# Scaling attention values in place for three of four head pairs, by GpSimd, instead of turning, scaling and turning back every block

## The chip, the cores and the metric

The kernel runs on one core of one Trainium2 chip. The metric is the device time of one execution in microseconds (us). The engines are named as in the profile: PE is TensorE (PEld its weight loads), DVE is VectorE, ACT is ScalarE, POOL is GpSimd, SP is SyncE, whose queue (SPq) issues all the DMAs of this kernel. Each engine works through its own instructions in the order in which they stand; between engines there are only semaphores.

## What is computed

There are 8 batches, 8 heads, 576 positions and 64 columns a head. Each head's attention keeps the 32 largest scores of a row, and its result goes, head beside head, into a mixer of width 512:

```python
scores = scale * np.matmul(q, k.transpose(0, 1, 3, 2))
kth = np.partition(scores, -top_k, axis=-1)[..., -top_k:-top_k + 1]
scores = np.where(scores >= kth, scores, -1000000000.0)
attn = np.exp(scores - np.max(scores, axis=-1, keepdims=True))
attn = attn / (np.sum(attn, axis=-1, keepdims=True) + 1e-09)
x = np.matmul(attn, v)            # then (B, S, H * D)
theta = x @ w_theta
zr, zi = x * np.cos(theta), x * np.sin(theta)
y = np.einsum('ts,bsd->btd', w_tok_r, zr) + np.einsum('ts,bsd->btd', w_tok_i, zi)
u = x + y
out = u + np.maximum(u @ w_ch, 0.0)
```

The division by the row's sum is what the change moves: both kernels multiply the values `attn @ v`, computed with unscaled weights, by the reciprocal of the sum.

## The kernel before

**Units.** Two heads make a pair; a batch has four pairs. A pair is worked on in five units, `j` = 0 to 4: four of 128 query rows for both heads, and a last one of the remaining 64 rows of both heads, which lie one under the other in the 128 partitions. For a unit the scores are made on PE (`scores`), copied by ACT, folded in two and searched for the 32nd largest value by DVE (`fold`, `pick`, `threshold`: rounds of MAX8 and MATCH_REPLACE8 on a list `lst`, of which there are three). POOL makes the limits from the list (`lim`, line 303) and a copy for a later check (`marks`, line 305); ACT makes a penalty (`pen`, line 311), POOL subtracts it (line 313), ACT takes the exponential with the row's sum (line 323), PE turns the result (`turn`), and PE multiplies it with the values (`mix_values`), which ACT keeps in `xt` (`keep_values`, line 378). `xt` has columns of heads in its 128 partitions (a pair for each of its four blocks) and the 576 positions along the row.

**The pipeline.** `pipeline` runs over 160 units, one step for each, and in each step it touches several neighbouring units at different stages. The loads of the next pair (`load_pair`, `split_pair`: `raw`, `hi`, `q`, `kh`, `kl`, `vt`, `vrem`) are written at the first two steps of a pair. All of it is then put in order by a scheduler, engine by engine, which works with its own estimates of durations; the program's text gives the priorities.

**The mixer.** When the last unit of a batch is kept, its `mixer` starts, a generator that is taken on by a few pieces in each step beside the units of the next batch; that of the last batch (with `split` set, in which PE works with high and low halves of its operands) has nothing beside it at the end. In its front part the sums have to be applied. A row's sum lies in the partition of its query position, while `xt` has the positions along the row. So for each block k of 128 positions (five, the last of 64) PE turns the four blocks of `xt` (`px_s`, line 542), DVE multiplies them by the reciprocals `rinv` into `xs` (`normalize`, line 443), and PE turns `xs` back (`px_t`, line 458), from where ACT copies it to `xt` (`turn_back`, line 459). `xs` is needed turned in any case, for the products with cosine and sine. Then come the angles (`angles`, PE, `pth`), their fraction (`fraction`), sine and cosine on ACT (`trig`), the products by POOL (lines 506 and 511), the matmuls over positions (`py`, line 585), and those over columns (`po`, line 610). The exponential and the sine need different tables on ACT, so that no exponential runs between the first sine and the last cosine of a mixer.

The reciprocals are made at the mixer's start from `sums` of all heads, [128, 5, 8], after POOL and ACT have moved the sums of the last units to the right partitions (lines 411 and 412), by DVE (lines 415 and 416).

Of the kernel before, what the change touches and what calls it, by code (L numbers as in the profile page):

```python
# [22 lines left out]
AHEAD = 2  # L23
S_LATE = 0
# [19 lines left out]
def topk_attention_phase_mixer(  # L44
# [33 lines left out]
    ps_m = ctx.enter_context(tc.tile_pool(name="ps_m", bufs=2, space=bass.MemoryType.PSUM))  # L78

# [10 lines left out]
    nc.gpsimd.memset(marks[:, :, 1:], 0.0)  # L90
    factors = const.tile([P, 1, 2], F32, name="factors")
# [287 lines left out]


# [28 lines left out]
    def mixer(bt, split=False):  # L409
        bq, xt, sums, sums_rem = bt["bq"], bt["xt"], bt["sums"], bt["sums_rem"]  # L410
        nc.gpsimd.tensor_copy(sums[:REM, NJ, 0::2], sums_rem[0:D])
        nc.scalar.copy(sums[:REM, NJ, 1::2], sums_rem[D:P])
        rinv = wk2.tile([P, NJ + 1, H], F32, tag="rinv", name="rinv")
# [23 lines left out]
        def normalize(k, px):  # L437
            rows, parts = (P, 1) if k < NJ else (REM, folds)
            for a in range(parts):
                cols = slice(a * DM // parts, (a + 1) * DM // parts)  # L440
                out = xs[a * D : a * D + rows, k, : DM // parts]
                hs = slice(cols.start // D, cols.stop // D)
                nc.vector.tensor_tensor(
                    out.rearrange("p (h d) -> p h d", d=D),
                    px[:rows, cols].rearrange("p (h d) -> p h d", d=D),
                    rinv[:rows, k, hs].unsqueeze(2).to_broadcast([rows, hs.stop - hs.start, D]),
                    op=ALU.mult,
                )

        def turn_back(j):  # L450
            rows, parts = (P, 1) if j < NJ else (REM, folds)
            m = NB // parts
            for a in range(parts):
                sl = slice(a * D, a * D + rows)
                pt = ps_t.tile([P, NB, P], F32, tag="t", name="px_t")
                with later(M_PE):
                    for p in range(m):
                        nc.tensor.transpose(pt[:, p, :rows], xs[sl, j, p * P : p * P + P], ident[sl, sl])
                nc.scalar.copy(xt[:, a * m : a * m + m, j * P : j * P + rows], pt[:, :m, :rows])  # L459
                if split:  # L460
                    cs = slice(j * P, j * P + rows)
                    nc.scalar.copy(x_hi[:, a * m : a * m + m, cs], pt[:, :m, :rows])
                    for p in range(a * m, a * m + m, 2):
                        pp = slice(p, p + 2)
                        nc.vector.tensor_sub(x_lo[p // 2][:, :, cs], xt[:, pp, cs], x_hi[:, pp, cs].bitcast(F32))
# [22 lines left out]
        def fraction(j):  # L488
            whole = wk2.tile([P, DM], F32, tag="whole", name="whole", bufs=1)
# [46 lines left out]
        for k in range(NJ + 4):  # L536
# [245 lines left out]
```

## Time and profile before

| | us |
|---|---|
| median of 3 runs | 1294.06 |
| lowest and highest | 1293.27 and 1298.52 |
| the profiled execution | 1298.9 |
| its span, from the first to the last instruction | 1297.1 |

| engine | busy, us | share of the span |
|---|---|---|
| PE | 1168.7 | 90% |
| DVE | 1165.8 | 90% |
| ACT | 1018.5 | 79% |
| POOL | 663.1 | 51% |

The profile is of the one execution, and it is 4.8 us above the median. The ends of matmuls are modelled, so that PE's busy time holds some overlap of one matmul with the next. A batch takes about 150 us: the tables of the exponential are loaded at 233.8, 380.6, 529.1, 681.7, 830.4, 981.5 and 1129.7 us, at the end of the sine and cosine of each batch but the last. The last mixer, alone, begins at about 1215 us.

### The profile page before, as it was taken

The numbers are of one execution on the slowest core, as the hardware profiler recorded it, in microseconds if no ns is written. First come the engines' busy times: TensorE is split into PE (matmuls) and PEld (weight loads), VectorE is DVE, ScalarE is ACT, GpSimd is POOL, SyncE is SP. The second block draws the span as 40 slices with busy tenths as digits, with TensorE's granted clock in tenths as the row PEclk, the third lists the DMA queues.
The fourth block names the chain that finished last, engine by engine and source line by source line (L and its number), as shares of the span: only waits on it lengthen the run. The fifth ranks groups of instructions, "written<-read, shape, count | busy, mean of one in ns | idle before, by whom it ended". The sixth has DMA issues, their size and how long they took to land.

```text
span 1297.1 us, 21711 instructions
## 1 busy us (share of the span) xinstructions
PE 1168.7 (90%) x6293; PEld 852.4 (66%) x6293; DVE 1165.8 (90%) x3993; ACT 1018.5 (79%) x2098; POOL 663.1 (51%) x784
## 2 busy tenths in 40 slices
PE   3676688899989999999989998899988999999998
PEld 3554455678657775578656775577756786577688
DVE  7999999999988899999998899999998799999353
ACT  5998888987788688787779778977778778887560
POOL 3667765654465345544455435554464444655440
PEclk9676789999999999899999999999999999999999
DMA  6244532322412342313413333123423233220001
GB/s 177 83 132 130 149 100 56 91 76 84 126 36 56 83 129 74 80 40 92 135 48 74 83 110 92 36 67 90 128 56 81 58 95 103 72 60 11 37 2 39
DMA packets 71008, 106.04 MB, mean 82 GB/s; under 512 B 13920, under 2 KB 32608, under 8 KB 70880
## 3 DMA queue, kind: packets, MB, share of 16 engines
q1 hardware_dynamic: 70880, 104.57, 29.5%
q8 instruction: 52, 0.85, 0.3%
q14 instruction: 76, 0.62, 0.2%
HBM read 38.40 MB, written 9.44 MB: 37 GB/s over the span
## 4 chain that ended last, share of the span: by engine, by line
DVE 32%; PE 32%; ACT 22%; POOL 4%; SPq 3%; issue 3%; DMA 3%; ACTq 0%; DVEq 0%; POOLq 0%
PE py L585 11%; DVE lst L292 10%; DVE lst L298 9%; PE pth L481 6%; PE px L366 4%; ACT e L323 4%; ACT pen L311 4%; DVE lst L274 3%; DVE lo L275 3%; DVE lst L279 3%; ACT e L252 3%; PE ps_score L243 3%; SPq L211 3%; ACT at L340 3%; PE pt L338 2%
## 5 line engine op out<-in xcount | busy, mean ns | idle before, releaser
L313 POOL TENSOR_TENSOR e<-e,pen 128x576 f32<-128x576 f32 x288 | 365.3, 1286 | 195.2 <-ACT pen L311 184.3
L292 DVE MAX8 lst<-lst 128x8 f32<-128x296 f32 (+3 forms) x1152 | 424.1, 406 | 0.9
L298 DVE MATCH_REPLACE8 lst<-lst 128x277 f32<-128x277 f32 (+2 forms) x864 | 329.2, 386 | 0.0
L585 PE MATMUL py<-w,z 128*128 128x288 f32 x1008 | 270.4, 412 | 0.0
L323 ACT ACTIVATE e<-e,lim 128x576 f32<-128x576 f32 x288 | 225.7, 786 | 34.7 <-POOL e L313 33.7
L311 ACT ACTIVATE pen<-e,lim 128x576 bf16<-128x576 f32 x288 | 211.0, 776 | 37.0 <-POOL lim L303 37.0
L243 PE MATMUL ps_score<-kh,q 128*128 128x288 f32 x512 | 186.3, 378 | 56.4 <-DVE lo L275 30.9
L585 PEld LDWEIGHTS py<-w,z 128*128 128x128 f32 x1008 | 184.7, 192 | 52.8 <-issue 5.4
L338 PE MATMUL pt<-ident,e 128*128 128x128 f32 x1152 | 176.8, 287 | 29.5 <-ACT at L340 15.0
L338 PEld LDWEIGHTS pt<-ident,e 128*128 128x128 f32 x1152 | 139.5, 146 | 71.2 <-ACT at L340 18.8
L366 PE MATMUL px<-at,vt 128*64 128x320 f32 (+1 forms) x1024 | 174.9, 440 | 4.5 <-ACT at L343 4.5
L252 ACT COPY e<-ps_score 128x576 f32<-128x576 f32 x256 | 163.1, 650 | 10.7 <-PE ps_score L243 10.2
L340 ACT COPY at<-pt 128x512 f32<-128x512 f32 x256 | 145.0, 589 | 29.5 <-PE pt L338 28.5
L243 PE MATMUL ps_score<-kl,q 128*128 128x288 f32 x512 | 155.4, 318 | 1.3 <-DMA kl<-raw 1.3
L243 PEld LDWEIGHTS ps_score<-kh,q 128*128 128x128 f32 x512 | 103.1, 201 | 77.7 <-DVE lo L275 28.1
L274 DVE TENSOR_TENSOR lst<-ps_score,e 128x576 f32<-128x576 f32 (+1 forms) x160 | 109.5, 685 | 47.8 <-ACT e L252 22.1
L366 PEld LDWEIGHTS px<-at,vt 128*64 128x64 f32 x1024 | 77.8, 145 | 72.2 <-issue 26.4
L610 PE MATMUL po<-xt,w 128*128 128x288 f32 x448 | 118.7, 408 | 0.7 <-DVE xt L566 0.3
L279 DVE MAX8 lst<-lo 128x8 f32<-128x288 f32 x288 | 116.6, 440 | 0.0
L481 PE MATMUL pth<-w,xt 128*128 128x512 f32 x224 | 107.3, 624 | 5.6 <-ACT xt L459 5.6
L275 DVE TENSOR_TENSOR lo<-ps_score,e 128x576 f32<-128x576 f32 (+1 forms) x160 | 109.5, 684 | 0.0
L243 PEld LDWEIGHTS ps_score<-kl,q 128*128 128x128 f32 x512 | 104.2, 204 | 7.1 <-issue 2.0
(120 smaller groups left out, 1689.1 us busy)
## 6 DMA issues: line engine op xcount, KB each, us to landing
kh<-hi SPq DMA_DIRECT2D x124, 144.0 KB, 2.7
kl<-raw SPq DMA_DIRECT2D x124, 144.0 KB, 2.6
raw<-in_qT_dram SPq DMA_DIRECT2D x31, 288.0 KB, 3.0
raw<-in_kT_dram SPq DMA_DIRECT2D x31, 288.0 KB, 3.1
q<-hi SPq DMA_DIRECT2D x62, 144.0 KB, 2.5
q<-raw SPq DMA_DIRECT2D x62, 144.0 KB, 2.7
vt<-in_v_dram SPq DMA_DIRECT2D x32, 256.0 KB, 2.8
out_dram<-ot SPq DMA_DIRECT2D x28, 288.0 KB, 2.1
```

Source lines behind the costliest of these rows:

```text
L243: nc.tensor.matmul(out[:, at : at + n], l, r, start=(i == 0), stop=(i == len(mm) - 1), skip_group_check=True)
L252: nc.scalar.copy(u.x[:, :, keys], u.ps[:, :, :HS])
L292: nc.vector.max(lst[:, w, best], part[w])
L298: nc.vector.match_replace(out=rest, in_to_replace=lst[:, w, best], in_values=part[w], imm_value=LOWEST)
L311: nc.scalar.activation(pen[:, w], u.x[:, w], AF.Relu, bias=u.lim[:, w, 0:1], scale=-STEEP)
L313: nc.gpsimd.tensor_sub(u.x[:, w], u.x[:, w], pen[:, w])
L323: nc.scalar.activation(u.x[:, w], u.x[:, w], AF.Exp, bias=u.lim[:, w, 1:2], scale=SCALE, accum_out=acc)
L338: nc.tensor.transpose(pt[:, c], e[:, w, at0 : at0 + P], ident)
L340: nc.scalar.copy(at[:, w, :, q0 : q0 + P], pt)
L366: nc.tensor.matmul(px[sl, :n], pr["vt"][:, kb, sl], pr["at"][:, a, kb], start=(kb == 0), stop=False, skip_group_check=True)
L481: nc.tensor.matmul(th[j][: l.shape[-1]], l, r, **pos)
L585: nc.tensor.matmul(py[:, :HS], l, r, start=(i == 0), stop=(i == len(mm) - 1))
```

## The change

For pairs 0, 1 and 2 of a batch the reciprocals are made beside the units of the next pair, and `xt` is scaled where it lies. `spread`, two steps after a pair's last unit: POOL adds 1e-9 to the pair's sums [128, 9], DVE takes the reciprocal, PE turns the 9 columns into rows, ACT copies these (`line`), three DMAs write them to memory as two rows of 576 (`away`), and two DMAs read each row back into 64 partitions (`wide`). `scale`, four steps after a pair's last unit: POOL multiplies the pair's block of `xt` [128, 576] by `wide` in place.

In the mixer only pair 3 is turned, multiplied by DVE and turned back (`turn_last`, `turn_back`). The other three pairs are turned once, for `xs`, and copied by ACT (`turn_values`). The fraction of the angles shares a buffer with the output `ot`. The mixer has nine pieces up to its sines' end, where it had ten.

```diff
+SPREAD = 4
+    far = ctx.enter_context(tc.tile_pool(name="far", bufs=2, space=bass.MemoryType.DRAM))
+    small = const.tile([P, 2 * NJ + 1], F32, name="small")
+    nc.vector.memset(small, 1e-9)
...
-            if j < NJ:
-                acc = bt["sums"][:, j, 2 * p + w : 2 * p + w + 1]
-            else:
-                acc = bt["sums_rem"][:, p : p + 1]
+            if j == 0 and w == 0:
+                bt["sums"][p] = wk2.tile([P, 2 * NJ + 1], F32, tag="sums", name="sums")
+            c = w * NJ + j if j < NJ else 2 * NJ
+            acc = bt["sums"][p][:, c : c + 1]
...
+    def invert(bt, p):
+        rinv = wk2.tile([P, 2 * NJ + 1], F32, tag="rinv", name="rinv")
+        nc.gpsimd.tensor_add(rinv, bt["sums"][p], small)
+        nc.vector.reciprocal(rinv, rinv)
+        return rinv
+    def spread(bt, p):
+        rinv = invert(bt, p)
+        pr = ps_t.tile([P, NJ * P], F32, tag="t", name="pr")[: 2 * NJ + 1, :P]
+        nc.tensor.transpose(pr, rinv, ident)
+        row = wk2.tile([2 * NJ + 1, P], F32, tag="line", name="line", bufs=1)
+        nc.scalar.copy(row, pr)
+        away = far.tile([2, S], F32, tag="away", name="away")
+        for w in range(2):
+            nc.sync.dma_start(away[w, : NJ * P].rearrange("(j q) -> j q", q=P), row[w * NJ : w * NJ + NJ])
+        nc.sync.dma_start(away[:, NJ * P :].unsqueeze(0), row[2 * NJ :].rearrange("o (w q) -> o w q", w=2))
+        wide = wk2.tile([P, S], F32, tag="wide", name="wide", bufs=1)
+        for w in range(2):
+            nc.sync.dma_start(wide[w * D : w * D + D], away[w].partition_broadcast(D))
+        bt["wide"][p] = wide
+    def scale(bt, p):
+        nc.gpsimd.tensor_mul(bt["xt"][:, p], bt["xt"][:, p], bt["wide"][p])
...
-        for rows, js in ((P, slice(0, NJ)), (REM, slice(NJ, NJ + 1))):
-            nc.vector.tensor_scalar(rinv[:rows, js], sums[:rows, js], 1e-9, None, op0=ALU.add)
-            nc.vector.reciprocal(rinv[:rows, js], rinv[:rows, js])
+        rinv = invert(bt, lp)
+        rrem = wk2.tile([P, 2], F32, tag="rrem", name="rrem")
+        nc.gpsimd.tensor_copy(rrem[:REM, :1], rinv[:D, 2 * NJ :])
+        nc.scalar.copy(rrem[:REM, 1:], rinv[D:, 2 * NJ :])
...
+        def turn_values(k):
+            rows = P if k < NJ else REM
+            px = ps_t.tile([P, DM], F32, tag="t", name="px_s")
+            with later(M_PE):
+                for p in range(lp):
+                    nc.tensor.transpose(px[:rows, p * P : p * P + P], xt[:, p, k * P : k * P + rows], ident)
+            if k < NJ or split:
+                nc.scalar.copy(xs[:rows, k, : lp * P], px[:rows, : lp * P])
...
+            for p in range(lp):
+                halve(u_hi[p], u_lo[p], xt[:, p], nc.scalar.copy, nc.vector.tensor_sub)
+        turn_last()
+        yield
+        turn_back()
+        turn_values(0)
+        yield
+        for k in range(NJ + 2):
             if k <= NJ:
...
+                angles(k)
+            if k < NJ:
+                turn_values(k + 1)
+            if k:
+                fraction(k - 1)
...
+            for gone, act in ((2, spread), (SPREAD, scale)):
+                u = unit(i - gone)
+                if u and u.j == NJ and u.p < NPAIR - 1:
+                    act(u.batch, u.p)
```

Line numbers of the changed kernel are four higher from the units on, and more in the mixer: the subtraction of the penalty is line 313 before and 317 now, `lim` 303 and 307, `marks` 305 and 309. Two places show what moved. The first is PE at the front of a batch's mixer, beside the scores (`ps_score`) of the next batch's first pair. Before, turning (`px_s`) and turning back (`px_t`) alternate, block by block:

```order
L542 MATMUL px_s<-ident,xt 128x128 x4
L458 MATMUL px_t<-ident,xs 128x128 x4
L243 MATMUL ps_score<-kh,q_6599 128x288
L243 MATMUL ps_score<-kl,q_6599 128x288
L243 MATMUL ps_score<-kh,q_6599 128x288
L243 MATMUL ps_score<-kl,q_6599 128x288
L338 MATMUL pt<-ident,e 128x128 x8
```

Now, at the same mixer, pair 3 is turned and turned back once for all blocks:

```order
L473 MATMUL px_s<-ident,xt 128x128 x4
L473 MATMUL px_s<-ident,xt 64x128
L247 MATMUL ps_score<-kh,q_6730 128x288
L247 MATMUL ps_score<-kl,q_6730 128x288
L247 MATMUL ps_score<-kh,q_6730 128x288
L247 MATMUL ps_score<-kl,q_6730 128x288
L495 MATMUL px_t<-ident,xs 128x128 x4
L495 MATMUL px_t<-ident,xs 128x64
```

Later in this mixer no `px_t` follows; for each of the five blocks there is one turn of the other three pairs (line 508).

The second place is POOL at the end of pair 3 of the fifth batch, where the mixer's reciprocals are prepared. Before:

```order
L303 TENSOR_TENSOR lim<-lst,factors 128x2
L313 TENSOR_TENSOR e<-e,pen 128x576
L411 COPY sums<-sums_rem 64x4
L305 COPY marks<-lst 128x10
L303 TENSOR_TENSOR lim<-lst,factors 128x4
L199 TENSOR_TENSOR raw<-raw,hi 128x1152
L313 TENSOR_TENSOR e<-e,pen 128x576 x2
```

Now the scaling of pair 2 (line 408) stands there, between `marks` and `lim` of the next batch's first unit:

```order
L307 TENSOR_TENSOR lim<-lst,factors 128x2
L317 TENSOR_TENSOR e<-e,pen 128x576
L386 TENSOR_TENSOR rinv<-sums,small 128x9
L443 COPY rrem<-rinv 64x1
L309 COPY marks<-lst 128x10
L408 TENSOR_TENSOR xt<-xt,wide 128x576
L307 TENSOR_TENSOR lim<-lst,factors 128x4
L317 TENSOR_TENSOR e<-e,pen 128x576 x2
L309 COPY marks<-lst 128x10
L203 TENSOR_TENSOR raw<-raw,hi 128x1152
```

So the multiplication is ahead of `lim`, and the subtraction for the loads (`raw`) has moved behind the penalties.

## Rows read from the trace of the kernel before

**Rows 1.** The page: busy time by engine, and the chain that ended last.

```profile
PE 1168.7 (90%) x6293; PEld 852.4 (66%) x6293; DVE 1165.8 (90%) x3993; ACT 1018.5 (79%) x2098; POOL 663.1 (51%) x784
...
DVE 32%; PE 32%; ACT 22%; POOL 4%; SPq 3%; issue 3%; DMA 3%; ACTq 0%; DVEq 0%; POOLq 0%
```

**Rows 2.** Windows: stretch, length, busy (count): PE PEld DVE ACT POOL; clock, DMA.

```profile
0.00:233.80 233.80, 162.47 (x757) 111.94 (x758) 221.58 (x759) 194.74 (x396) 145.62 (x167) 0.79 0.41 116
...
681.70:830.40 148.70, 140.78 (x772) 101.18 (x771) 137.24 (x480) 120.92 (x249) 75.34 (x92) 1.00 0.31 82
...
1215.00:1297.10 82.10, 73.79 (x491) 64.67 (x489) 33.48 (x63) 35.31 (x69) 20.42 (x14) 0.98 0.06 24
```

**Rows 3.** Groups by line and shape, DVE: count | busy us, mean ns | idle before.

```profile
L443 DVE TENSOR_TENSOR xs<-px_s,rinv 128x512 f32<-128x512 f32 x32 | 21.4, 670 | 2.3 <-PE px_s L542 2.3
...
L443 DVE TENSOR_TENSOR xs<-px_s,rinv 64x256 f32<-64x256 f32 x14 | 5.7, 410 | 0.1
...
L415 DVE TENSOR_SCALAR rinv<-sums 128x32 f32<-128x32 f32 x8 | 4.2, 530 | 0.0
...
L416 DVE RECIPROCAL rinv<-rinv 128x32 f32<-128x32 f32 x8 | 2.7, 338 | 0.0
...
L415 DVE TENSOR_SCALAR rinv<-sums 64x8 f32<-64x8 f32 x8 | 2.4, 305 | 1.2 <-POOL sums L411 1.2
...
L416 DVE RECIPROCAL rinv<-rinv 64x8 f32<-64x8 f32 x8 | 1.4, 176 | 0.0
```

**Rows 4.** The chain that ended last, from 1170 us: start us, us, what.

```profile
1227.31 0.44 PE px_s L542 x4
...
1230.04 0.59 PE px_s L542 x4
```

**Rows 5.** What ended idle time before instructions that touch `px_t`: us, times.

```profile
  DVE xs L443: 15.3, 15
```

**Rows 6.** Groups by line and shape, ACT's copies from PSUM and one POOL product.

```profile
L459 ACT COPY xt<-px_t 128x512 f32<-128x512 f32 x32 | 18.9, 591 | 8.1 <-PE px_t L458 7.7
...
L343 ACT COPY at<-pt 128x256 f32<-128x256 f32 x64 | 21.1, 390 | 4.0 <-PE pt L338 3.8
...
L354 ACT COPY rem<-pq 64x64 f32<-64x64 f32 x64 | 13.3, 209 | 7.1 <-PE pq L351 6.1
...
L152 POOL TENSOR_TENSOR w<-room 128x576 f32<-128x576 f32 x9 | 12.9, 1437 | 0.1
```

**Rows 7.** POOL's timeline at the fifth batch's last unit: start, us, what, [idle before].

```profile
762.99 0.18 POOL L411 COPY sums<-sums_rem 64x4 f32<-64x4 f32 x1 [0.97 <-ACT e L323]
764.09 0.20 POOL L305 COPY marks<-lst 128x10 f32<-128x10 f32 x1 [0.92 <-DVE lst L292]
765.53 0.20 POOL L303 TENSOR_TENSOR lim<-lst,factors 128x4 f32<-128x4 f32 x1 [1.24 <-DVE lst L302]
767.29 2.65 POOL L199 TENSOR_TENSOR raw<-raw,hi 128x1152 fp32r<-128x1152 f32 x1 [1.56 <-ACT hi L198]
769.90 2.53 POOL L313 TENSOR_TENSOR e<-e,pen 128x576 f32<-128x576 f32 x2
```

**Rows 8.** SP's timeline, four issues in the fourth batch's mixer.

```profile
682.42 2.38 SPq L518 DMA_DIRECT2D z<-whole  x4
```

**Rows 9.** Waits over the span: who waited for what, us, times, longest.

```profile
DVE lst L274 <- POOL lim L303: 20.5, 12, 4.4
...
ACT qpad L224 <- DMA q<-raw: 16.1, 14, 2.8
```

**Rows 10.** DMA issues: count, KB each, median us from issue to landing.

```profile
kh<-hi SPq DMA_DIRECT2D x124, 144.0 KB, 2.7
...
z<-whole SPq DMA_DIRECT2D x28, 64.0 KB, 2.0
```

**Rows 11.** Line 383 on DVE: count, ns min/median/max, first and last start.

```profile
L383 DVE TENSOR_TENSOR z_lo<-z,z_hi x9: 679/949/1567, 1243.0 to 1259.3; 128x512 fp32r<-128x512 f32 x9
...
L383 DVE TENSOR_TENSOR w<-w,w_hi x4: 670/692/693, 1226.3 to 1229.3; 128x512 fp32r<-128x512 f32 x4
```

More of the change, by code (lines that the diff above doesn't have):

```diff
@@ L435, in spots @@
             return xs[:, NJ, :HD], last[0][:, :HD], last[0][:, HD:]
[L437 to L455, printed above, removed]
-                with later(M_PE):
-                    for p in range(m):
-                        nc.tensor.transpose(pt[:, p, :rows], xs[sl, j, p * P : p * P + P], ident[sl, sl])
-                nc.scalar.copy(xt[:, a * m : a * m + m, j * P : j * P + rows], pt[:, :m, :rows])
-                if split:
[L461 to L465, printed above, removed]
+        def turn_last():
+            mine = xs[:, :, lp * P :]
+            for c in range(2):
+                pt = ps_t.tile([P, NJ, P], F32, tag="t", name="px_s")
+                js, rows = (range(NJ), P) if c == 0 else ((NJ,), REM)
+                with later(M_PE):
+                    for i, j in enumerate(js):
+                        nc.tensor.transpose(pt[:rows, i], xt[:, lp, j * P : j * P + rows], ident)
+                if c == 0:
+                    out = xs[:, :NJ, lp * P :].rearrange("p j (w d) -> p j w d", d=D)
+                    by = rinv[:, : 2 * NJ].rearrange("p (w j) -> p j w", w=2).unsqueeze(3).to_broadcast([P, NJ, 2, D])
+                    nc.vector.tensor_mul(out, pt.rearrange("p j (w d) -> p j w d", d=D), by)
+                else:
+                    out = place(lp).rearrange("p (w d) -> p w d", d=D)
+                    by = rrem[:REM].unsqueeze(2).to_broadcast([REM, 2, D])
+                    nc.vector.tensor_mul(out, pt[:REM, 0].rearrange("p (w d) -> p w d", d=D), by)
@@ new lines, in place, with turn_back @@
+        def place(p):
+            a, c = (0, p) if split else divmod(p, NPAIR // 2)
+            return xs[a * D : a * D + REM, NJ, c * P : c * P + P]
+        def turn_back():
+            for c in range(2):
+                pt = ps_t.tile([P, NJ, P], F32, tag="t", name="px_t")
+                js, rows = (range(NJ), P) if c == 0 else ((NJ,), REM)
+                sl = slice(0, P) if c == 0 else slice(0, REM) if split else slice(D, D + REM)
+                with later(M_PE):
+                    for i, j in enumerate(js):
+                        src = xs[:, j, lp * P :] if c == 0 else place(lp)
+                        nc.tensor.transpose(pt[:, i, :rows], src, ident[sl, sl])
+                cs = slice(js[0] * P, js[0] * P + len(js) * rows)
+                flat = pt.rearrange("p j q -> p (j q)")[:, : len(js) * rows]
+                nc.scalar.copy(xt[:, lp, cs], flat)
+                if split:
+                    nc.scalar.copy(x_hi[:, lp, cs], flat)
+                    nc.vector.tensor_sub(u_lo[lp][:, cs], xt[:, lp, cs], u_hi[lp][:, cs].bitcast(F32))
@@ L535, in mixer @@
             z_lo.append(wk2.tile([P, S], F32R, tag="lo1", name="z_lo")[:, :DM])
[L536 to L550 removed]
+            for p in range(lp):
[6 more added lines that the diff above has]
+        for k in range(NJ + 2):
+            if k <= NJ:
+                angles(k)
[3 more added lines that the diff above has]
+                fraction(k - 1)
+            if k <= NJ:
                 yield
@@ L732, in plain_batch @@
                 prev = u
+            if p < NPAIR - 1:
+                spread(bt, p)
+                scale(bt, p)
         for _ in mixer(bt):
```

28 lines of the change are left out of this document (7 added, 21 removed).

## The prediction

> **What bounds the kernel now.** I read the engines' busy times first, then the chain that ended last, then the busy time by stretch. DVE and PE are both busy for 90% of the span, ACT for 79%, POOL for 51% [rows 1]. The chain passes through DVE and PE for 32% each, ACT 22%, POOL 4% [rows 1]. By stretch it is plainer [rows 2]: in the first 233.8 us DVE is busy for 221.6; in a steady batch of 148.7 us DVE has 137.2, PE 140.8 (its ends are modelled), ACT 120.9, POOL 75.3; only in the last 82.1 us is DVE slack (33.5) and PE alone the bound (73.8). So nearly everywhere DVE and PE are full together. Work taken from both is worth most, work given to ACT some of its length, work given to POOL little, as long as nobody waits for POOL.
>
> **The change part by part.**
>
> *DVE.* Out go the multiplications of all blocks, 21.4 + 5.7 us, and the reciprocals' preparation, 4.2 + 2.7 + 2.4 + 1.4 us [rows 3]: 37.8 us in eight batches. In come 32 reciprocals of 128x9, each between the 176 ns of 64x8 and the 338 ns of 128x32 [rows 3]; I take 176, the nearer size, so 5.6 us (10.8 at most). Eight multiplications of 128x512 at 670 ns are 5.4 us, eight of 64x128 at no more than the 410 ns of 64x256 are 3.3 us. The last batch's subtractions for the low halves are cut otherwise but cover the same elements. Net: 37.8 - 14.3 = 23.5 us less, 2.9 us a batch.
>
> *PE.* A mixer now has 40 turns (20 there, 20 back). It will have 5 + 5 for pair 3 and 15 for the others, and the three small ones of `spread`: 28. That is 12 fewer in each batch, 96 in all. In the chain four of them take 0.44 to 0.59 us [rows 4], so 0.11 to 0.15 each: 10.6 to 14.2 us less; I take 12.4. DVE's multiplications ended 15.3 us of PE's idle time ahead of `px_t` in 15 places [rows 5]; matmul and weight load are both counted in it, so about half is time. Two of five such trips stay in a mixer, so I count 4 us more.
>
> *ACT.* Four copies of 128x512 at 591 ns, two of 128x128 and one small one go, about 3.1 us a batch. In come one copy of 128x512 and one of 128x64 (0.8 together), four of 128x384, whose mean lies between 390 and 591 ns (0.49 taken, 2.0 us) [rows 6], two for the rest (0.39 and 0.3), three for `line` at between 0.21 and 0.39 (0.3 taken) and one small one: 4.6 us. Net 1.5 us more a batch, 11 us in all (8 to 14).
>
> *POOL.* Three products of two f32 operands, 128x576, at 1437 ns [rows 6], and four additions of 128x9 at about the 0.20 us of `lim` [rows 7], against one copy that goes and one that comes: 5.1 us more a batch, 41 us in all. Half of POOL's time is free [rows 1].
>
> *SP.* Five DMAs for each of 24 pairs, 120 issues of 0.6 us (four took 2.38 us [rows 8]). The first three wait for ACT's `line`, the last two for the landing of the first three. Behind them on SP's queue stand the loads of the next pair (`raw`, `q`, `kh`, `kl`), 3 us of issue and some 2 us of waiting later than now. Those loads are a pair ahead; I cost this at nothing, and at up to 2.8 us a pair where ACT already waits for `q` [rows 9].
>
> *From the two bound engines to the end.* If DVE's 23.5 and PE's 12.4 us arrive by each engine's part in the chain, 32 of 90, it is 0.36 x 35.9 = 13 us. If both engines stay as full as now, the smaller saving carries the larger one where they are full together, and DVE's extra part counts only in the first batch and where PE waits for it: 12.4 to 23.5 us. I take 14, and the 4 us of the trips: 18 us less. ACT's 11 us count by 22/79, 3 us; POOL's 41 us by 4/51, 3 us more.
>
> *The new wait.* This is the part that no row shows. The product on POOL needs `wide`, and `wide` comes by way of memory: the copy to `line` (0.3), two issues before the third of the first group starts (1.2), its landing (2.0, as for `z<-whole`), one issue of the second group before the last starts (0.6), and its landing (2.7, as for `kh<-hi`, equal in size) [rows 8, 10]: 6.8 us from ACT's copy to POOL's product. In 6 of the 24 places the order puts ACT's copy right behind the last exponential of a pair, and POOL's product right behind the addition or the copy that waits for that same exponential, ahead of the next unit's `lim`, as in the second place shown with the change. Laid over the trace of now: the exponential ends at about 763.0, `lim` runs at 765.53, the penalties' subtraction at 769.90 [rows 7]. With the product, `wide` would land at 769.8, the product end at 771.2, and `lim` come 5.7 us late; since `raw` (2.65 us) no longer stands ahead of the subtraction, and ACT needs some 1.5 us for the penalties in between, the subtraction would come some 3 us late. What is queued behind: `lim`, the subtraction, then the exponential on ACT and the turn on PE; DVE meets it when a new list needs the buffer that `lim` still reads, a unit later. The bounds for the end are 0 (the exponential comes earlier than now, or the lists' slack of one unit covers it) and 6 x 5.7 = 34 us. The same scheduler's estimate for loads is mostly good: of ACT's 64 copies from `q` 14 waited, 16.1 us in all [rows 9]. Where `lim` was late, DVE lost 20.5 us in 12 places, 1.7 each [rows 9]. I take 3 us, two of the six places at that price, since most readers of a load that this scheduler placed did not wait.
>
> Sum: -18 + 3 + 3 + 3 = **-9 us**. The profiled execution's 1298.9 would become 1289.9; it lies 4.8 us above the median, near the highest of three runs, so I set the sum against the median: **1285 us**.
>
> *A rule weighed.* DVE's subtraction of two operands in SBUF took 670 to 693 ns while POOL stood idle and up to 1567 ns beside POOL's products [rows 11]. The Trainium skill, "SBUF — State Buffer", section "Who interferes with whom", says that a DVE instruction with two SBUF inputs and a GpSimd instruction that reads SBUF shut each other out, whereas a DVE instruction with at most one SBUF input is not touched. The trace agrees [rows 11]. By that rule POOL's 24 products leave DVE's searches alone, and the three new low-half subtractions of the last batch, which read SBUF twice, could each be held by the row's 0.9 us: the sum would be -6 and the time 1288; without the rule it is -9.
>
> **The rivals.**
>
> *The saving arrives whole.* For it: in the steady batch DVE is the longer bound of the two wherever PE's ends are only modelled, and turning back no longer stands between the sums and the angles. Then DVE's 23.5 us count fully, ACT's and POOL's additions hide, no wait passes on, and the sum is -18 to -26: 1268 to 1276, taken 1272. Against it: PE is as full as DVE [rows 2].
>
> *GpSimd waits for the way through memory, and the units wait for GpSimd: slower.* The place is POOL's queue between a pair's last exponential and the next `lim`. If the 6 tight places cost 3 us each, as the subtraction's lateness says, and the four or five where the product stands just behind the sines' end, or behind one unit's subtractions, cost 2 to 3 us, it is 18 + 12 = 30 us; against the saving of 18 and with ACT's and POOL's 6 us, +18: 1312; with lesser lateness 1301. It decides from 12 us of waiting that reach DVE or PE. For it: 6.8 us of way against 2.5 us between `sums` and `lim` [rows 7, 8, 10]. Against it: a list's buffer of slack, and the order of the rest being made anew around it.
>
> *Nothing arrives.* PE's saving falls into places where it waits for DVE's `lo` or ACT's copies, and ACT, at 81% of the batch, takes over: 1294, within 5 us.
>
> **How the numbers follow.** My forecast, 1285 (1278 to 1292 by itself), gets 0.45; the whole saving 0.17; slower by GpSimd's wait 0.26; nothing 0.12. A measurement of this kernel can tell about 0.5%, 6.5 us, from no change: faster is below 1287.6, slower above 1300.5. Of the forecast's own spread two thirds lie below 1287.6. Faster: 0.17 + 0.30 = 0.47; same: 0.15 + 0.10 = 0.25; slower: 0.26 + 0.02 = 0.28. The range from 1269 to 1308 leaves out the far end of the whole saving (0.04) and the upper half of the slower rival (0.13).
>
> **What would show it.** Right: DVE's busy time falls to about 1142 us, PE's turns by 96, POOL rises to about 704, ACT to about 1030; the stretch from one exponential's table to the next shrinks from 149 to about 148 us; POOL's product waits for `wide` under 1 us on the average; the idle time before `px_t` falls by more than half. Wrong towards slower: among the waits "POOL xt <- DMA wide" with 3 us or more in several places, and behind it more of "DVE lst <- POOL lim" or "PE pt <- ACT e" than now. Wrong towards faster: a batch below 146.5 us. If DVE's busy time falls and the batch stays at 149, PE or ACT was the bound; then the idle time of DVE, by what ended it, names which.

## The result, and the profile after

The changed kernel takes **1309.5 us** (median of six runs, 1304.2 to 1313.0) where the kernel before, beside it, takes 1293.8: a ratio of **1.0117** (95% interval 1.0094 to 1.0139). It is 1.2% slower. The forecast was 1285, and the range ended at 1308. Of the rivals, "GpSimd waits" (1312, with lesser lateness 1301) comes nearest.

Page of the changed kernel's profile, busy time and chain (against [rows 1]):

```profile
PE 1164.4 (89%) x6197; PEld 854.2 (65%) x6197; DVE 1149.7 (88%) x3958; ACT 1020.8 (78%) x2138; POOL 701.2 (54%) x840
...
PE 47%; ACT 19%; DVE 18%; DMA 5%; issue 4%; SPq 4%; POOL 3%; ACTq 0%; POOLq 0%; DVEq 0%
```

The work moved the way that was counted: PE has 96 instructions fewer and is busy for 4 us less, DVE for 16 us less, ACT for 2 us more, POOL for 38 us more. The span grew all the same, so engines stand idle. The six batches between the loads of the exponential's table at the end of the first mixer's sines and of the seventh's tell where. Windows of before, then of after; columns as in [rows 2]:

```profile
233.81:1129.75 895.94, 850.29 (x4617) 614.66 (x4616) 839.85 (x2941) 723.52 (x1496) 451.43 (x550) 0.99 0.31 82
```

```profile
236.29:1142.20 905.91, 847.76 (x4554) 615.71 (x4554) 824.55 (x2899) 723.53 (x1525) 476.09 (x590) 0.98 0.32 87
```

DVE's busy time falls by 15.3 us there, but its idle time rises from 56.1 to 81.4 (length less busy). The difference of the two, 10.0 us, is by its making the growth of these batches; the whole span grew by 10.7 us between these two executions, so nearly all of it lies here.

Groups of the changed kernel (columns as in [rows 3]): the product, the additions, the reciprocals, and DVE's multiplications for pair 3:

```profile
L408 POOL TENSOR_TENSOR xt<-xt,wide 128x576 f32<-128x576 f32 x24 | 33.9, 1414 | 57.8 <-DMA wide<-away 52.1 <-ACT at L344 2.6 <-PE py L633 2.0
L386 POOL TENSOR_TENSOR rinv<-sums,small 128x9 f32<-128x9 f32 x32 | 6.6, 205 | 25.3 <-ACT e L327 25.3
L387 DVE RECIPROCAL rinv<-rinv 128x9 f32<-128x9 f32 x32 | 6.5, 203 | 3.6 <-POOL rinv L386 3.6
L477 DVE TENSOR_TENSOR xs<-px_s,rinv 128x512 f32<-128x512 f32 x8 | 5.5, 685 | 6.0 <-PE px_s L473 6.0
...
L481 DVE TENSOR_TENSOR xs<-px_s,rrem 64x128 f32<-64x128 f32 x8 | 2.3, 283 | 3.3 <-PE px_s L473 3.1
```

POOL stands 52.1 us ahead of 14 of its 24 products for the row from memory. What ended idle time before instructions that touch `px_t`, in the view of [rows 5], now reads:

```profile
  DVE xs L481: 3.8, 4
  DVE xs L477: 2.1, 4
```

That is 5.9 us in place of 15.3, which was the aim. Waits of the kernel before, then of the changed kernel (who waited for what, us, times, longest; see [rows 9]):

```profile
ACT pen L311 <- POOL lim L303: 37.0, 30, 3.6
...
DVE lst L274 <- ACT e L252: 22.1, 17, 5.2
...
PE pt L338 <- ACT e L323: 13.3, 13, 1.9
...
DVE lst L274 <- ACT e L263: 3.1, 3, 1.1
```

```profile
ACT pen L315 <- POOL lim L307: 53.7, 34, 4.2
POOL xt L408 <- DMA wide<-away: 52.1, 14, 8.8
...
DVE lst L278 <- ACT e L256: 27.6, 22, 3.3
...
PE pt L342 <- ACT e L327: 21.0, 13, 5.2
...
DVE lst L278 <- POOL lim L307: 17.7, 11, 4.5
DVE lst L278 <- ACT e L267: 16.9, 9, 2.8
```

One of the tight places, the whole way of a row, all engines (start, us, what; against [rows 7]):

```profile
463.49 0.20 POOL L386 TENSOR_TENSOR rinv<-sums,small 128x9 f32<-128x9 f32 x1 [1.13 <-ACT e L327]
...
465.62 0.25 ACT L397 COPY line<-pr 9x128 f32<-9x128 f32 x1
466.63 0.77 SPq L400 DMA_DIRECT2D away<-line  x2
467.45 0.64 SPq L401 DMA_DIRECT2D away<-line  x1
469.39 1.09 SPq L404 DMA_DIRECT2D wide<-away  x2
474.19 1.42 POOL L408 TENSOR_TENSOR xt<-xt,wide 128x576 f32<-128x576 f32 x1 [8.78 <-DMA wide<-away]
475.71 0.20 POOL L307 TENSOR_TENSOR lim<-lst,factors 128x4 f32<-128x4 f32 x1
475.94 1.44 ACT L315 ACTIVATE pen<-e,lim 128x576 bf16<-128x576 f32 x2 [4.17 <-POOL lim L307]
```

From the start of ACT's copy to that of the product it is 8.6 us here. In the 14 places where a product stood for the row it is 6.3 to 8.6 us, with a median of 6.8. Behind the product `lim` is late, and ACT stands 4.2 us for it.

### The profile page after: what moved, and what is told of

It reads as the page before. It is cut to its first block, busy times and chain, and to the rows that moved or that the text cites. A ratio compares the mean times of both kernels' runs of the same rounds, so it can differ in the third digit from the quotient of the medians.

```text
span 1307.8 us, 21733 instructions
## 1 busy us (share of the span) xinstructions
PE 1164.4 (89%) x6197; PEld 854.2 (65%) x6197; DVE 1149.7 (88%) x3958; ACT 1020.8 (78%) x2138; POOL 701.2 (54%) x840
## 4 chain that ended last, share of the span: by engine, by line
PE 47%; ACT 19%; DVE 18%; DMA 5%; issue 4%; SPq 4%; POOL 3%; ACTq 0%; POOLq 0%; DVEq 0%
PE py L633 16%; PE px L370 8%; PE ps_score L247 6%; DVE lst L296 6%; PE pth L529 5%; DVE lst L302 5%; PE po L658 5%; PE pt L342 4%; ACT e L327 3%; ACT e L256 3%; SPq L215 3%; ACT pen L315 3%; DVE lst L278 2%; DVE lo L279 2%; DVE lst L283 2%
## 5 line engine op out<-in xcount | busy, mean ns | idle before, releaser
L296 DVE MAX8 lst<-lst 128x8 f32<-128x277 f32 (+3 forms) x1152 | 421.3, 407 | 1.1
L315 ACT ACTIVATE pen<-e,lim 128x576 bf16<-128x576 f32 x288 | 210.1, 775 | 53.9 <-POOL lim L307 53.7
L342 PE MATMUL pt<-ident,e 128*128 128x128 f32 x1152 | 181.8, 290 | 30.4 <-ACT e L327 21.0
L342 PEld LDWEIGHTS pt<-ident,e 128*128 128x128 f32 x1152 | 143.0, 148 | 66.5 <-ACT e L327 27.9
L370 PE MATMUL px<-at,vt 128*64 128x320 f32 (+1 forms) x1024 | 180.2, 455 | 5.4 <-ACT at L347 4.6
L247 PE MATMUL ps_score<-kl,q 128*128 128x288 f32 x512 | 159.1, 325 | 5.9 <-DMA kl<-raw 5.9
L370 PEld LDWEIGHTS px<-at,vt 128*64 128x64 f32 x1024 | 82.8, 151 | 74.0 <-issue 26.7
L247 PEld LDWEIGHTS ps_score<-kl,q 128*128 128x128 f32 x512 | 105.4, 206 | 13.5 <-issue 6.8
L203 POOL TENSOR_TENSOR raw<-raw,hi 128x1152 fp32r<-128x1152 f32 x31 | 82.1, 2648 | 41.7 <-ACT hi L202 38.5
```

The lines of the kernel that those rows point to most:

```text
L247: nc.tensor.matmul(out[:, at : at + n], l, r, start=(i == 0), stop=(i == len(mm) - 1), skip_group_check=True)
L296: nc.vector.max(lst[:, w, best], part[w])
L315: nc.scalar.activation(pen[:, w], u.x[:, w], AF.Relu, bias=u.lim[:, w, 0:1], scale=-STEEP)
L342: nc.tensor.transpose(pt[:, c], e[:, w, at0 : at0 + P], ident)
L370: nc.tensor.matmul(px[sl, :n], pr["vt"][:, kb, sl], pr["at"][:, a, kb], start=(kb == 0), stop=False, skip_group_check=True)
```

## The experiments

All figures are ratios to the kernel before on the same chip, with 95% intervals.

### One thing taken away, the order made anew

Some of these kernels leave steps out, so that the values of three pairs stay unscaled or are scaled wrongly; they serve for timing alone.

**e1_const**: the product takes a constant instead of the row.

```diff
-        nc.gpsimd.tensor_mul(bt["xt"][:, p], bt["xt"][:, p], bt["wide"][p])
+        nc.gpsimd.tensor_mul(bt["xt"][:, p], bt["xt"][:, p], marks.rearrange("p a b -> p (a b)")[:, :S])
```

> The product on POOL takes a tile that is always there in place of the row from memory; the reciprocals, the turn, the copy and all five DMAs a pair are still made, but nothing reads what they bring, so the values of three pairs are scaled wrongly. Waits theory (POOL's product stands 52 us in all for the row, and limits and the loads' subtraction behind it come late): POOL's idle time ahead of the product falls from 58 us to under 8, time 1283 to 1296. Queue theory (five more DMAs a pair hold up the next pair's loads on SP): the DMAs stay, so 1303 to 1311. Work theory (24 products and ACT's copies cost by their own length): 1303 to 1311. Mixer theory (the new order of the mixer is what loses): 1303 to 1311.

Measured 0.9939 (0.9921 to 0.9958).

**e2_noprod** and **e3_none**: no products; and neither products nor rows.

```diff
-            for gone, act in ((2, spread), (SPREAD, scale)):
+            for gone, act in ((2, spread),):      # e2_noprod
+            for gone, act in ():                  # e3_none
```

> Only the 24 products on POOL are left out, so three pairs' values stay unscaled; reciprocals, turns, copies and DMAs stay. Waits theory: 1280 to 1294, within 6 us of the run with the constant tile. Work theory: 1283 to 1292 here, and 10 us or more below the run with the constant tile. Queue theory and mixer theory: 1303 to 1311.

> Neither reciprocals, turns, copies and DMAs for three pairs nor their products: three pairs' values stay unscaled, only the new mixer is left. This is the most that the change could bring. Waits theory: 1277 to 1290, at most 6 us below the run without products. Queue theory: 15 us or more below the run without products, 1280 to 1292. Mixer theory: still 1298 or more, since the loss is in the mixer.

Measured 1.0046 (1.0019 to 1.0072) for e2_noprod and 0.9897 (0.9853 to 0.994) for e3_none.

**e5_early**: the turned row takes a buffer of the scores (`ps_s`) instead of one of the turned weights (`ps_t`), so that it needn't stand behind the pair's last turns; all is computed.

```diff
-        pr = ps_t.tile([P, NJ * P], F32, tag="t", name="pr")[: 2 * NJ + 1, :P]
+        pr = ps_s.tile([P, 2, 512], F32, tag="s", name="pr")[: 2 * NJ + 1, 0, :P]
```

> The changed kernel, all of it computed, but the nine columns are turned into one of the two buffers of the scores instead of one of the two of the turned weights, so that the turn does not stand behind all turns of its pair; the copy and the DMAs then start 3 to 9 exponentials earlier in the order, while the product stands where it stood. Waits theory: idle time ahead of the product from 58 us to under 20, time 1283 to 1297. Queue, work and mixer theories: no gain, 1303 to 1313, since all work and all DMAs are still there.

Measured 0.9965 (0.994 to 0.9991). The new mixer alone gains 1%, so the loss comes with the scaling. But e2_noprod is a miss that spoils the reading of the rest: e1_const has the same instructions and 24 products more, and is 1% faster. The scheduler makes a new order for each edit: laid side by side, the traces of these two have nearly half of TensorE's instructions in other places.

### The same order with and without the wait

From here on an order is held fixed: the program is laid out twice, and in the second pass each instruction is tied behind the one that stood ahead of it on its engine in the first. The traces bear it out: apart from the scaling's own steps, f1_after_order and g3_none_after_order have the changed kernel's order on PE, DVE, ACT, POOL and SP.

```diff
+    PRODUCT = "wide"
+    nc, arrays = built(None)
...
+    order = [i.name for i in max(blocks, key=lambda b: len(b.instructions)).instructions]
+    PRODUCT = "ones"
+    nc, arrays = built(order)
```

**f1_after_order** (above): the changed kernel's order, no wait for the row. **f4_tiny**: the same with products of 8 columns. **f5_free**: the constant in both passes. **f2_free_order**: the constant in the first pass, the row in the second.

> Left out: the values are multiplied by a constant one (96 columns read six times) in place of the row from memory, so they stay unscaled; every transfer is still made, and every engine has its instructions in exactly the order of the changed kernel, fixed by a first pass in which the product reads the row. Only the wait for the row is gone. Before 1298, changed 1309.5 in earlier runs. Waits theory (the 52 us for which GpSimd stands before the products is what costs): 1287 to 1294, and the products wait for nothing but the kept values. Order theory (what costs is that the scheduler, which knows of the round trip, placed the other instructions elsewhere; half of TensorE's rows stand in other places than without it): 1303 to 1311. Both half: 1296 to 1302.

> Left out: as f1_after_order, in the changed kernel's order and without the wait for the row, and the product takes 8 columns instead of 576 (values unscaled). Against f1_after_order only the 24 products' work is gone (33.9 us busy on GpSimd). Work theory (GpSimd's own 1.41 us per product pushes the next limits back): 8 to 20 us below f1_after_order. Waits theory and order theory: within 4 us of f1_after_order.

> Left out: the product multiplies by the constant one (values unscaled), in the order that the scheduler makes for that; all transfers made. The fourth corner: neither the wait for the row nor an order made with it in view. It should repeat the kernel whose product took 576 columns of another constant (1289.7): 1286 to 1294 by both theories. If it comes out above 1298, the order of the scheduler alone moves the time by more than the effects under study.

> Nothing left out: the changed kernel, all scaled by the row from memory, but every engine has its instructions in the order that the scheduler makes when the product needs no row. So the wait for the row is there in an order that is blind to it. Waits theory: the product stands close behind the last kept value and waits longer than in the changed kernel, over 52 us, so 1309 to 1325. Order theory: 1290 to 1300, though the product waits.

| | order made without the row | order made with it |
|---|---|---|
| product waits for the row | f2_free_order 1.0542 (1.0514 to 1.0571) | changed kernel 1.0117 (1.0094 to 1.0139) |
| product takes a constant | f5_free 1.0002 (0.9987 to 1.0018) | f1_after_order 1.0017 (1.0003 to 1.003) |

f4_tiny gave 1.0021 (0.9996 to 1.0046): the products' 33.9 us of work cost nothing that shows. The wait costs 1.0% in the changed kernel's order, some 13 us, and 5.4% in an order that is blind to it. Waits of f2_free_order, then of f5_free, which has the same order:

```profile
POOL xt L419 <- DMA wide<-away: 133.0, 20, 14.5
...
DVE lst L282 <- ACT e L260: 70.7, 32, 6.5
...
ACT pen L319 <- POOL lim L311: 63.4, 22, 7.7
```

```profile
POOL xt L419 <- ACT xt L386: 39.8, 14, 6.8
DVE lst L282 <- ACT e L260: 32.9, 20, 6.5
...
ACT pen L319 <- POOL lim L311: 16.4, 14, 2.6
```

With the wait for the row two others grow by 47 and 38 us: that of ACT's penalties for `lim`, and that of DVE for ACT's copies of the scores. So GpSimd's wait is passed on to the units. The changed kernel shows the same, smaller: ACT's penalties wait 39.5 us for `lim` in f1_after_order and 53.7 in the changed kernel, and DVE stands idle in the six batches for 73.6 and 81.4 us. The six batches and the first stretch of f1_after_order, then the first stretch of the changed kernel:

```profile
232.94:1130.64 897.70, 844.01 (x4558) 614.18 (x4558) 824.06 (x2899) 724.99 (x1524) 477.77 (x589) 0.98 0.33 88
0.00:232.94 232.94, 157.56 (x725) 111.65 (x725) 220.03 (x760) 194.88 (x400) 152.28 (x176) 0.82 0.44 119
```

```profile
0.00:236.29 236.29, 161.73 (x725) 112.97 (x725) 220.68 (x759) 195.11 (x401) 152.05 (x177) 0.77 0.43 117
```

Of the 10.8 us between these two executions 8.2 lie in the six batches. Another 3.4 lie in the first stretch, where the products hardly wait (0.1 us) and TensorE's granted clock was 0.77 on the average against 0.82. So a part of the 13 us may be the clock's. No run holds the clock fixed, but it does not rank the kernels: over the span it was 0.933 to 0.948 in the runs of g3_none_after_order (1.0036) and 0.934 to 0.947 in those of e5_early (0.9965).

Order theory and waits theory had each half for f1_after_order: without the wait the changed kernel's order still lacks the mixer's gain. But f5_free is a miss for both. It should have repeated e1_const (0.9939), and its order, made without the row in view, lacks the gain as well. So an order can lose the gain without having the row in view.

### What is left, taken away step by step in the changed kernel's order

The product takes the constant in all four; in **g8_no_transfers** the five DMAs are left out, in **g9_only_reciprocals** the turn and ACT's copy too, in **g3_none_after_order** all of it. **g2_no_waits** leaves nothing out, but lets each step read constants. The last, in short:

```diff
+        nc.gpsimd.tensor_add(rinv, small if free else bt["sums"][p], small)
...
+        nc.tensor.transpose(pr, ident[:, : 2 * NJ + 1] if free else rinv, ident)
...
+        row = ident[: 2 * NJ + 1] if free else row
```

> All four kernels of this group have every remaining instruction in the changed kernel's own order, and the product takes the constant one as in f1_after_order (1.0017 of the kernel before; the kernel with the new mixer alone, in an order of its own, 0.990). Left out here: the 120 transfers of the row (values unscaled). Queue theory (SP holds the loads of raw, vt and weights behind transfers that wait for line): 0.990 to 0.996. Buffer theory (the turned row takes one of the two buffers of the turned weights, and holds TensorE up until ScalarE has copied it): within 0.003 of 1.0017. Addition theory (GpSimd stands 25 us before its additions until the pair's last exponential): within 0.003 of 1.0017. Order theory: within 0.003 of 1.0017.

> Left out: the transfers, and the turn of the reciprocals and ScalarE's copy of it (values unscaled). GpSimd's additions, VectorE's reciprocals and the product by one are kept. Buffer theory: 0.990 to 0.995 here, and 0.999 or more in g8_no_transfers. Queue theory: the same as g8_no_transfers within 0.003. Addition and order theory: still 0.999 or more.

> Left out: all of the three pairs' scaling (additions, reciprocals, turns, transfers, products; values unscaled). What stays is what the kernel with the new mixer alone has, but in the order that the changed kernel has for it. Order theory: 0.998 to 1.004, as f1_after_order. The other theories: 0.988 to 0.993, as the same instructions in their own order. In between, the order costs the difference to 0.990 and the scaling's own steps the difference to 1.0017.

> Nothing left out in number, but no step of the scaling waits for another engine's data: the additions add two constants, the turn takes columns of the unit matrix, the transfers take its rows, the product the constant one (values unscaled). The turn still takes its buffer, and ScalarE still copies it. Addition theory and queue theory: 0.990 to 0.996. Buffer theory and order theory: within 0.003 of 1.0017.

Measured 1.0056 (1.0039 to 1.0074), 1.0049 (1.0024 to 1.0074), 1.0036 (1.0012 to 1.0059) and 1.0039 (1.0022 to 1.0056), all near f1_after_order's 1.0017. g8_no_transfers and g9_only_reciprocals lie just above the 0.003 that the order theory allowed around it, with less to do; f1_after_order ran on another chip than these four, so differences of 0.4% are not read here. Nothing gains by being taken away: neither SP's queue, nor the turned row's hold on its buffer, nor the additions' waits show a cost by themselves there. g3_none_after_order has the very instructions of e3_none, and is 1.4% slower by their order. What the tying itself costs was not measured, as no kernel was tied to its own order; but tied kernels with the same instructions differ by 1.8% (below), so the order matters without it. The six batches of e3_none, then of g3_none_after_order:

```profile
228.38:1112.74 884.36, 843.46 (x4553) 616.27 (x4554) 824.70 (x2906) 720.37 (x1509) 448.86 (x556) 0.98 0.31 84
```

```profile
237.15:1139.42 902.27, 849.73 (x4540) 616.65 (x4540) 823.70 (x2881) 722.26 (x1506) 448.70 (x553) 0.97 0.31 81
```

DVE's work is equal, its idle time 59.7 and 78.6 us. The groups suggest an early link: ACT's copies of the turned weights (`at`) wait more for their turns. e3_none, then g3_none_after_order:

```profile
L344 ACT COPY at<-pt 128x512 f32<-128x512 f32 x256 | 145.0, 589 | 15.0 <-PE pt L342 13.5 <-PE ps_score L247 0.9
```

```profile
L349 ACT COPY at<-pt 128x512 f32<-128x512 f32 x256 | 146.0, 588 | 38.3 <-PE pt L347 36.9
```

And DVE waits more for ACT's copies of the scores, which ACT makes too; its waits in the six batches of e3_none, then of g3_none_after_order:

```profile
DVE lst L278 <- POOL lim L307: 13.4, 10, 2.7
DVE lst L278 <- ACT e L267: 9.3, 6, 2.1
DVE lst L278 <- ACT e L256: 7.9, 12, 1.9
```

```profile
DVE lst L283 <- ACT e L261: 23.9, 17, 3.1
DVE lst L283 <- POOL lim L312: 16.7, 10, 4.6
DVE lst L283 <- ACT e L272: 14.5, 8, 2.8
```

### A bad draw, or the row's buffer?

The instructions of e3_none in three more orders: **n3_other_draw** (24 added copies on DVE, which nobody reads, shuffle it), **g11_none_early_order** (the order of e5_early), **g12_none_second_order** (the order of e2_noprod).

```diff
+            for gone, act in ((2, nudge),):       # n3_other_draw
...
+        nc.vector.tensor_copy(t, small)
```

> Left out: all of the three pairs' scaling (values unscaled), as in the kernel with the new mixer alone, which gave 0.990 of the kernel before. Added: 24 copies of 128x9 on VectorE into a tile that nobody reads, some 0.1 to 0.2 us each and waiting for nothing. They do nothing, but a quarter of TensorE's rows and a third of VectorE's come to stand elsewhere by them. If an order is a draw, with a spread of some half per cent whatever made it: 0.986 to 1.004, and anything over 0.996 speaks for it. If only the scaling's steps make a bad order: 0.989 to 0.994.

> Left out: all of the three pairs' scaling (values unscaled). The rest stands in the order of the kernel whose turned row has a buffer of the scores (0.9965 with everything computed). In the changed kernel's order the same instructions took 1.0036, in their own 0.990. If the order is what made that kernel better than the changed one: 0.988 to 0.994. If it was only its shorter wait for the row: 0.999 to 1.004, as in the changed kernel's order.

> Left out: all of the three pairs' scaling (values unscaled). The rest stands in the order of the kernel that made and sent the row but had no products (1.0046), which differs from the changed kernel's order in a third of TensorE's rows; in both orders the turned row has one of the two buffers of the turned weights. The same instructions took 1.0036 in the changed kernel's order, 0.990 in their own, 0.993 in the draw with idle copies, 0.985 in the order with the row's buffer among the scores. If orders made around a turned row in that pool are worse: 0.998 to 1.006. If the changed kernel's order is one bad draw: 0.985 to 0.994.

| order made for | the same instructions take |
|---|---|
| row in `ps_t`, changed kernel (g3) | 1.0036 (1.0012 to 1.0059) |
| row in `ps_t`, no products (g12) | 1.0037 (1.0019 to 1.0055) |
| no row (e3) | 0.9897 (0.9853 to 0.994) |
| no row, added copies (n3) | 0.9928 (0.9908 to 0.9948) |
| row in `ps_s` (g11) | 0.9853 (0.9822 to 0.9885) |

Both orders made around a turned row in the pool of the turned weights are worse than all three others by 1% or more. The copies of n3_other_draw were not as idle as expected:

```profile
L409 DVE COPY nudge<-small 128x9 f32<-128x9 f32 x24 | 16.0, 733 | 0.0
```

The shortest took 0.15 us; one that started during a GpSimd subtraction for the loads took up to 2.46 us, until that ended. So 0.9928 has up to 16 us of DVE's work in it beside the order.

In g12_none_second_order ACT's copies again wait for their turns, in g11_none_early_order less:

```profile
L349 ACT COPY at<-pt 128x512 f32<-128x512 f32 x256 | 146.9, 590 | 38.8 <-PE pt L347 37.3
```

```profile
L349 ACT COPY at<-pt 128x512 f32<-128x512 f32 x256 | 144.0, 589 | 26.0 <-PE pt L347 25.0
```

That link is not shown to be the cause: g11_none_early_order is the fastest of the five, and its copies wait longer than those of e3_none (25.0 against 13.5 us). Nor is the pool a strict rule: e1_const (0.9939) and f5_free (1.0002) have such orders too, each with the scaling's steps in it, so draws differ by half a per cent besides. What in an order makes it slow stays open.

These orders tell one thing more. The scaling's steps cost 0.8% in the changed kernel's order (1.0117 against 1.0036) and 1.1% in that of e5_early (0.9965 against 0.9853). So e5_early is better than the changed kernel by its order, 1.8% for the bare instructions, and the runs do not show that it makes the scaling cheaper, though its products stand only 6.5 us for the row.

### Versions that keep the result

**i1_late_no_addition** leaves GpSimd's addition of 1e-9, which a sum of at least one does not feel in float32, out of the changed kernel, **e11_no_addition** does it on top of e5_early. **p6_pinned** writes the product two steps later and ties it behind all that GpSimd has been given by then.

```diff
-        nc.gpsimd.tensor_add(rinv, bt["sums"][p], small)
-        nc.vector.reciprocal(rinv, rinv)
+        nc.vector.reciprocal(rinv, bt["sums"][p])
...
-SPREAD = 4
+SPREAD = 6                                        # p6_pinned
-        nc.gpsimd.tensor_mul(bt["xt"][:, p], bt["xt"][:, p], bt["wide"][p])
+        tc.keep_in_program_order(nc.gpsimd.tensor_mul(bt["xt"][:, p], bt["xt"][:, p], bt["wide"][p]))
```

> Nothing left out: the changed kernel with its products two units later in the program and each tied behind all that GpSimd was given before it, so that some of them start when the row has long landed. The changed kernel's order without the wait gave 1.0017, with it 1.0117. Waits theory: the products' idle time falls from 52 us to 30 to 40, and the time to 1.004 to 1.010. Order theory adds a draw of plus or minus 0.005 to that.

> Nothing left out but the added 1e-9, which a sum of at least one in float32 doesn't feel. The kernel with the turned row in a buffer of the scores (0.9965), without GpSimd's additions: VectorE inverts the sums themselves. GpSimd loses its 29.6 us of waits before the additions. Addition theory: 0.988 to 0.993. Order theory: GpSimd's waits there cost nothing by themselves (taking all of them away gave 1.0039 after 1.0017), so 0.992 to 1.002, as the order falls.

> Nothing left out but the added 1e-9. The changed kernel (1.0117) without GpSimd's additions; the turned row stays in the pool of the turned weights. With the row's buffer among the scores, leaving the additions out brought 0.9965 to 0.9875. If the additions (and their waits for the last exponential) cost that by themselves: 1.000 to 1.005 here. If they cost only through the order and the row's pool: 1.007 to 1.014. The wait for the row decides between: it should still be 35 to 50 us.

Measured: p6_pinned 1.008 (1.0061 to 1.0098), i1_late_no_addition 1.0063 (1.0037 to 1.0088), e11_no_addition **0.9875** (0.9854 to 0.9896), 1280.0 us: better than both kernels. What POOL's products wait for in e11_no_addition, and its six batches:

```profile
POOL xt L407 <- ACT xt L382: 26.0, 12, 7.8
...
POOL xt L407 <- DMA wide<-away: 4.5, 1, 4.5
```

```profile
234.09:1113.14 879.05, 839.81 (x4579) 614.83 (x4578) 824.85 (x2916) 727.07 (x1526) 473.17 (x565) 0.98 0.33 90
```

The wait for the row is 4.5 us instead of 52.1, and DVE stands idle for 54.2 us instead of 81.4. In p6_pinned the products wait 20.5 us for the row, less than the 30 to 40 expected, and a third of the loss is gone. In i1_late_no_addition, with the row still in `ps_t`, the wait for it stays 45.3 us, and half of the loss stays; its 1.0063 lies between the two ranges expected. Whether the additions cost anything by themselves, or their absence only draws a better order, is open: g2_no_waits says that their waits cost nothing in the changed kernel's order.

## Why the prediction was wrong

*What held.* The work: PE 96 turns fewer; on DVE the three new groups cost 6.5 + 5.5 + 2.3 us, the 14.3 counted, if by luck, as the reciprocals took more (203 ns for 176) and the small multiplications less (283 ns for 410); POOL's product 1414 ns for the 1437 taken, and its total +38 for +41. The place of the new wait: the six tight places held 35.5 of the products' 57.8 us of idle time. The way through memory: a median of 6.8 us from ACT's copy to the products that waited, 6.8 forecast. SP's 120 issues at nothing (g8_no_transfers). The saving: e3_none gives 13 us (8 to 19) for the 18 of the sum, but the same instructions gave 19 less to 5 more than the kernel before in the five orders tried, so no saving can be named without an order.

*Busy times.* DVE's fell by 16 instead of 23.5: 15.3 in the six batches, 2.6 a batch for the 2.9 forecast, and next to nothing in the first and the last. PE's fell by 4.3 for the 12.4 counted in the changed kernel, and by 12.3 in f1_after_order with the same instructions in the same order; half of the 8 us between these two lies in the first stretch, at the lower clock shown above.

*The step that failed first* is "I take 3 us" for the new wait, between bounds of 0 and 34. It costs about 13 us (changed kernel against f1_after_order; by the ends of the two intervals 8 to 18). The reason given, that most readers of a load which this scheduler placed did not wait, came from loads that are a pair ahead; here 14 of 24 waited, for the landing of five transfers in two steps. The slower rival had the steps right: POOL stands, `lim` is late, the units wait; and 13 us is just over its "12 us of waiting that reach DVE or PE". But it put 30 us on the wait, and that its 1312 lies so near 1309.5 is luck: the rest came from the order.

*The step that was missing* is the order of all the rest. The text named "the order of the rest being made anew around it" as a reason against the slower rival. It was the other half of the loss: g3_none_after_order against e3_none, 1.4%, 18 us (9 to 27 by the ends of the intervals). That takes the order of e3_none as the mark; against the slowest and the fastest of the other orders it is nothing to 24 us. Of the two signs that the text named, "DVE lst <- POOL lim" fell from 20.5 to 17.7 us, and "PE pt <- ACT e" rose from 13.3 to 21.0, but by the order: it is 21.4 in f1_after_order, where the product does not wait. The two waits of `lst` for ACT's `e`, which the text did not name, rose from 25.2 to 44.5, and to 39.4 without the wait for the row.

*Small terms.* POOL's +3 was too much: f4_tiny shows the products' work to be free in that order. ACT's busy time rose by 2 us for the 11 counted; what that costs no run isolates. The sum by the runs is then -13 for the mixer, +18 for the order, -2.5 for the scaling's other steps (f1_after_order against g3_none_after_order, within the noise) and +13 for the wait: +15.5, where +15.7 was measured. These are steps from one run to the next, so that they add up is no proof of them; each stands on its own pair of runs.

*The rule weighed*, the Trainium skill, "SBUF — State Buffer", section "Who interferes with whom": GpSimd's products should leave DVE's searches, with one operand in SBUF, alone. The trace agrees as far as it goes, with products beside a few of the searches only; searches of before and of after, 406 and 407 ns:

```profile
L292 DVE MAX8 lst<-lst 128x8 f32<-128x296 f32 (+3 forms) x1152 | 424.1, 406 | 0.9
```

```profile
L296 DVE MAX8 lst<-lst 128x8 f32<-128x277 f32 (+3 forms) x1152 | 421.3, 407 | 1.1
```

What the prediction drew from it for the three new low-half subtractions, that each could be held by 0.9 us, came true. They read SBUF twice, ran beside GpSimd's subtractions for the weights, and took 1663 ns each, where the same shape took 754 ns while GpSimd stood idle:

```profile
L413 DVE TENSOR_TENSOR x_lo<-xt,x_hi 128x576 fp32r<-128x576 f32 x3 | 4.8, 1663 | 1.3 <-ACT x_hi L412 1.3
...
L196 DVE TENSOR_TENSOR kl<-twice,kh 128x576 fp32r<-128x576 f32 x2 | 1.4, 754 | 6.0 <-ACT kh L195 6.0
```

That this cost the whole anything is not shown: the stretch that holds them, from the last load of the exponential's table to the end, went from 167.4 to 165.5 us.

## What to carry to other kernels

Where a scheduler lays out the program, an edit has two prices, that of its own steps and that of the new order; hold the order fixed and take the steps out, or the one is read as the other. Where a rare small step takes its buffer from is worth a try, since it changes the whole order: another pool gave 0.9965 for 1.0117 here. That the pool is the reason is not shown; with the old one, and no wait for the row, e1_const had 0.9939. A row sent by way of memory took 6.3 to 8.6 us here from the copy to the reader, so the copy must be early, or the engine that waits for it holds up everything queued behind.

## What was unexpected

An engine with half its time free can be given 34 us of products and feel nothing (1.0017 and 1.0021 with and without them), yet 52 us of standing in the same queue cost about 13 us of the whole. And the 120 transfers that share SP's queue with the loads cost nothing that shows in that order (1.0017 with them, 1.0056 without). The order alone moved the same instructions from 0.9853 to 1.0037, more than the whole change did.
